# Transposing attention weights by DMA instead of TensorE, with exponentials emitted earlier, in a top-k attention + MLP kernel

## The chip, the cores and the metric

The kernel runs on one core of a Trainium2 chip. The core has a matrix engine (PE, whose weight loads the profile lists as PEld), a vector engine (DVE), an activation engine (ACT), GpSimd (POOL) and a sync engine (SP), whose queue issues the DMAs. Each engine works off its own queue in order and waits on semaphores. The metric is device time in microseconds of one execution; lower is better.

## What is computed

Shapes: q, k and v are (8, 8, 576, 64), that is 8 batches of 8 heads; `w_in` is (512, 2048) and `w_out` (2048, 512), all float32.

```python
scores = scale * q @ k.T                        # 576 x 576 per head
kth    = np.partition(scores, -32)[..., -32]    # the 32nd largest of a row
scores = np.where(scores >= kth, scores, -1e9)
attn   = exp(scores - max) ; attn /= sum + 1e-9
x      = (attn @ v), heads joined               # 4608 tokens x 512
h      = x @ w_in                               # 4608 x 2048
g      = h if h >= 1, 0 if h <= -1, else (h + 1)**2 / 4
out    = g @ w_out                              # 4608 x 512
```

## The kernel before

**Steps.** Attention is cut into 144 steps. A step treats two sets of 128 query rows (128 queries of two heads, or the 64 left-over queries of four), so that its score tile `s` is 128 x 2 x 576. In a step PE makes the scores (L258, each float32 product is two MATMUL records), ACT copies them from PSUM (`s`, L261). DVE then finds the threshold of each row: it takes the larger of each pair (`more`, L269), four times the eight largest (MAX8, L283) with three MATCH_REPLACE8 between them (L292), then deals with the smaller halves (L297, L300, L301, L304). ACT makes the exponentials (`e`, L287) from the first maximum; DVE multiplies them by the mask and sums them (L312) and takes the reciprocal (L318). In the first 12 steps the reciprocals go into a diagonal matrix (`diag`, L322), and PE transposes and scales in one product (L342, L349). In the other 132 POOL scales the weights (L325), and PE transposes them block by block against the identity (L344 eight blocks, L352 one), with ACT copying the result to SBUF (`wT`, `wTt`, L345, L353). PE multiplies with v (L364, L372), and ACT copies the result to `xT` (L377).

**MLP.** When a chunk of one or two 128-token tiles is done, `hidden` makes 16 blocks of h in PSUM (`ph`, L394). ACT makes `r` and `g` from it (L398, L412), POOL finishes the activation with three instructions (L413 to L415), `final` multiplies with `w_out` (`py`, L422), ACT copies (L426) and SP stores. Only the very last chunk uses ACT and DVE instead of POOL (L403 to L405).

**Order.** The order on PE, DVE, ACT and POOL is written out by hand: a Python loop over the steps m, seven slots in each. `weights` is a generator whose yields spread a step's DVE work over the slots, `begin_at` emits scores, `transpose_w` and `values_until` the transposes and the products with v, and `advance` takes MLP work from the queue `pending`. A planner keeps estimated clocks: `dve_time` (a step takes `K_TIME`), `pe_time` (an MLP unit takes `UNIT_TIME`), and `until`, the time of the slot. While the MLP weights are being prepared (`early`, the first 12 steps), scores and values come in slots 4 and 2; later they both come at the start of a step. SP issues in the order written, too.

Of the kernel before, what the change touches and what calls it, by code (L numbers as in the profile page):

```python
# [10 lines left out]
F32 = mybir.dt.float32  # L11
U32 = mybir.dt.uint32
# [11 lines left out]
def kernel(  # L24
# [23 lines left out]
    SH = S // 2  # L48
    NK = DM // P
# [11 lines left out]
    nc.gpsimd.memset(minus, -1.0)  # L61
    two = const.tile([P, 1], F32, name="two")
# [32 lines left out]
    def load(pool, i):  # L95
        if i < n_pieces and i not in loaded:
            if room and i < 28:
                loaded[i] = room[i % 8]
            else:
                loaded[i] = pool.tile([P, 2 * WC], U32, name="raw", bufs=3)  # L100
            nc.sync.dma_start(out=loaded[i], in_=pieces_of_weights[i][1].bitcast(U32))

    def words_of(pool, i):
        load(pool, i)
        words = loaded.pop(i).rearrange("p (n t) -> p n t", t=2)
        return words[:, :, 0], words[:, :, 1]
# [31 lines left out]
    def inspect_piece(pool, i):  # L138

        _, hi = words_of(pool, i)  # L140
        for x in range(2):
            sign = pool.tile([P, WC], F32, name="sign", bufs=3)
# [4 lines left out]
    def run(ctx, paired):  # L147
        xtp = ctx.enter_context(tc.tile_pool(name="xtp", bufs=3))
        stage = ctx.enter_context(tc.tile_pool(name="stage", bufs=2))
        att = ctx.enter_context(tc.tile_pool(name="att", bufs=2))  # L150
        ps = ctx.enter_context(tc.tile_pool(name="ps", bufs=1, space=PSUM))
# [119 lines left out]
        def weights(st, after):  # L271
            s, m = st["s"], st["m"]
            tops = att.tile([P, 2, TOP_K + 8], F32, name="tops", bufs=3)
            st["e"] = e = att.tile([P, 2, S], F32, name="e")
            nmax = att.tile([P, 2], F32, name="nmax")
            kth = att.tile([P, 2, 8], F32, name="kth", bufs=3)
# [4 lines left out]
            for r in range(0, TOP_K, 8):  # L281
                for i in range(2):
                    nc.vector.max(out=tops[:, i, r:r + 8], in_=src[:, i, :])  # L283
                if r == 0:
                    nc.scalar.activation(nmax, tops[:, :, 0], AF.Copy, scale=-1.0)
                    for i in range(2):
                        nc.scalar.activation(e[:, i, :], s[:, i, :], AF.Exp, bias=nmax[:, i:i + 1])  # L287
                        if i == 0:
                            yield
                if r + 8 < TOP_K:  # L290
                    for i in range(2):
                        nc.vector.match_replace(out=rest[:, i, :], in_to_replace=tops[:, i, r:r + 8],  # L292
                                                in_values=src[:, i, :], imm_value=LOWEST)
                    src = rest
                yield
# [12 lines left out]
            if paired and after is not None:  # L308
                pairs(after)
# [9 lines left out]
            if st["by_tensor"]:  # L319
                st["rz"] = diag = att.tile([P, 2, P], F32, name="diag", bufs=1)  # L320
# [12 lines left out]
        def transpose_w(st):  # L333
            w = st["e"]
            st["wT"] = wT = att.tile([P, 2, NT, P], F32, name="wT", bufs=1)
            st["wTt"] = wTt = att.tile([P, P], F32, name="wTt", bufs=1)
            for i in range(2):
                pt = ps.tile([P, NT, P], F32, name="pw", tag="a", bufs=4)
                for c in range(NT):
                    w_in_place = w[:, i, main(i)][:, c * P:(c + 1) * P]  # L340
                    if st["by_tensor"]:
                        nc.tensor.matmul(pt[:, c, :], w_in_place, st["rz"][:, i, :], start=True, stop=True)  # L342
                    else:
                        nc.tensor.transpose(pt[:, c, :], w_in_place, ident)  # L344
                nc.scalar.copy(wT[:, i], pt)  # L345
            pt = ps.tile([P, P], F32, name="pwt", tag="a", bufs=4)
            if st["by_tensor"]:
                for i in range(2):
                    nc.tensor.matmul(pt[i * TL:(i + 1) * TL, :], w[:, i, tail(i)], st["rz"][:, i, :],  # L349
                                     start=True, stop=True)  # L350
            else:
                nc.tensor.transpose(pt, w.rearrange("p i n -> p (i n)")[:, SM:SM + P], ident)  # L352
            nc.scalar.copy(wTt, pt)  # L353


        def values(st):
            t, hp, v_in, v_tl = st["t"], st["hp"], st["keys"]["v"], st["keys"]["v_tl"]
            wT, wTt = st["wT"], st["wTt"]
            po = ps.tile([P, P], F32, name="po", tag="ph", bufs=3)
            if t < NT:  # L360
                for c in range(NT + 1):
                    for j in range(2):
                        h = 2 * hp + j
                        nc.tensor.matmul(po[j * D:(j + 1) * D], v_in[:, h, c, :] if c < NT else v_tl[0][:, h, :],  # L364
                                         wT[:, j, c, :] if c < NT else wTt, start=(c == 0), stop=(c == NT))
            else:
                for i in range(2):
                    cols = slice(i * TL, (i + 1) * TL)
                    for c in range(NT + 1):
                        for j in range(2):  # L370
                            h = 2 * (hp + i) + j
                            nc.tensor.matmul(po[j * D:(j + 1) * D, cols], v_in[:, h, c, :] if c < NT else v_tl[1][:, h, :],  # L372
                                             wT[:, i, c, j * TL:(j + 1) * TL] if c < NT else wTt[:, j * TL:(j + 1) * TL],
# [14 lines left out]
        def mlp(xT, tiles, pool, last):  # L388
            gs, pys = {}, {}

            def hidden(f, c0, c1):
# [6 lines left out]
                nc.scalar.activation(r, ph, AF.Relu, bias=half, scale=0.5)  # L398
# [3 lines left out]
                if last:  # L402
                    nc.vector.tensor_scalar(g, ph, -1.0, 0.0, ALU.add, ALU.max)  # L403
                    nc.scalar.activation(r, r, AF.Square)
                    nc.vector.scalar_tensor_tensor(out=g, in0=r, scalar=1.0, in1=g, op0=ALU.min, op1=ALU.add)  # L405
                    return
                if converted < n_pieces and f % 2:
                    nc.scalar.activation(r, r, AF.Square)
                    nc.scalar.activation(g, ph, AF.Relu, bias=minus, scale=1.0)
                    nc.gpsimd.tensor_scalar(r, r, 1.0, 0.0, ALU.min, ALU.max)  # L410
                else:
                    nc.scalar.activation(g, ph, AF.Relu, bias=minus, scale=1.0)  # L412
                    nc.gpsimd.tensor_scalar(r, r, 1.0, 0.0, ALU.min, ALU.max)  # L413
                    nc.gpsimd.tensor_tensor(out=r, in0=r, in1=r, op=ALU.mult)  # L414
                nc.gpsimd.tensor_tensor(out=g, in0=r, in1=g, op=ALU.add)  # L415
# [26 lines left out]
        for b in range(0, B, 2):  # L442
# [4 lines left out]
            else:  # L447
                rounds += a + [tl, (b + 1, NT)] + c
                chunks += [a[0:2], a[2:4], [tl], c[0:2], c[2:3], c[3:4]]
# [9 lines left out]
        EARLY_CHUNKS = 4  # L459
# [110 lines left out]
        for i in range(2):  # L570
            load(mlp_pool, i)
# [134 lines left out]
```

## Time and profile before

| | |
|---|---|
| median of 3 runs | 1746.03 us (1745.57 to 1747.68) |
| profiled execution: its own time | 1746.35 us |
| profiled execution: span of the instructions | 1744.5 us, mean granted PE clock 0.982 |
| busy: PE, DVE, ACT, POOL | 1639.4, 1537.0, 1083.2, 946.9 us |
| DMA | 74.63 MB, q1 14.5% of 16 engines' span |

Busy times are unions of the records of an engine, so a busy engine can still be waiting in part. A wait is read from the side of the engine that stands idle: "DVE e L312 <- ACT e L287" is time in which DVE had nothing else to do than wait for ACT's line 287.

### The profile page before, as it was taken

The numbers are of one execution on the slowest core, as the hardware profiler recorded it, in microseconds if no ns is written. First come the engines' busy times: TensorE is split into PE (matmuls) and PEld (weight loads), VectorE is DVE, ScalarE is ACT, GpSimd is POOL, SyncE is SP. The second block draws the span as 40 slices with busy tenths as digits, with TensorE's granted clock in tenths as the row PEclk, the third lists the DMA queues.
The fourth block names the chain that finished last, engine by engine and source line by source line (L and its number), as shares of the span: only waits on it lengthen the run. The fifth ranks groups of instructions, "written<-read, shape, count | busy, mean of one in ns | idle before, by whom it ended". The sixth has DMA issues, their size and how long they took to land.

```text
span 1744.5 us, 33535 instructions
## 1 busy us (share of the span) xinstructions
PE 1639.4 (94%) x10665; PEld 1151.5 (66%) x10665; DVE 1537.0 (88%) x4875; ACT 1083.2 (62%) x2942; POOL 946.9 (54%) x1668
## 2 busy tenths in 40 slices
PE   5588989999999999999999999999999999999998
PEld 4476575667766757476756767567667666666665
DVE  7999979888899999999987999999997998899752
ACT  6688575676667857576655647556555555466452
POOL 5689183665544817264646645436365554555550
PEclk7799999999999999999999999999999999999999
DMA  8333112111121112111200101000010000000000
GB/s 253 116 98 97 46 30 65 44 43 41 42 63 52 44 49 65 46 49 41 62 13 22 25 22 44 17 24 17 23 39 19 19 10 14 13 7 7 7 7 15
DMA packets 116668, 74.63 MB, mean 43 GB/s; under 512 B 87296, under 2 KB 95488, under 8 KB 116480
## 3 DMA queue, kind: packets, MB, share of 16 engines
q1 hardware_dynamic: 116480, 72.37, 14.5%
q8 instruction: 87, 1.43, 0.3%
q14 instruction: 101, 0.83, 0.2%
HBM read 62.91 MB, written 9.44 MB: 41 GB/s over the span
## 4 chain that ended last, share of the span: by engine, by line
PE 65%; DVE 14%; POOL 11%; ACT 6%; issue 3%; DMA 0%; POOLq 0%; DVEq 0%; SPq 0%; ACTq 0%
PE py L422 25%; PE ph L394 18%; PE sp L258 7%; PE po L364 7%; PE pw L344 5%; DVE tops L283 4%; DVE more L292 3%; POOL g L415 3%; POOL r L414 3%; DVE e L312 3%; POOL e L325 2%; POOL r L413 2%; ACT s L261 1%; DVE seconds L300 1%; ACT r L398 1%
## 5 line engine op out<-in xcount | busy, mean ns | idle before, releaser
L394 PE MATMUL ph<-xT,w_in 128*128 128x128 f32 (+1 forms) x3200 | 558.0, 326 | 14.4 <-ACT g L412 13.2
L422 PE MATMUL py<-w_out,g 128*128 128x512 f32 x1152 | 530.9, 600 | 2.0 <-ACT y L426 2.0
L394 PEld LDWEIGHTS ph<-xT,w_in 128*128 128x128 f32 x3200 | 472.3, 192 | 87.9 <-ACT g L412 26.0
L325 POOL TENSOR_SCALAR e<-e,rz 128x576 f32<-128x576 f32 x264 | 195.0, 750 | 520.2 <-DVE rz L318 488.8
L283 DVE MAX8 tops<-more 128x8 f32<-128x288 f32 x1152 | 465.4, 445 | 0.0
L292 DVE MATCH_REPLACE8 more<-tops,more 128x288 f32<-128x288 f32 x864 | 375.6, 442 | 0.0
L422 PEld LDWEIGHTS py<-w_out,g 128*128 128x128 f32 x1152 | 205.2, 190 | 224.1 <-issue 215.8
L312 DVE SCALAR_TENSOR_TENSOR e<-s,kth,e 128x576 f32<-128x576 f32 x288 | 245.7, 881 | 116.6 <-ACT e L287 116.3
L398 ACT ACTIVATE r<-ph,half 128x128 f32<-128x128 f32 (+1 forms) x400 | 166.5, 416 | 216.8 <-POOL g L415 156.7
L415 POOL TENSOR_TENSOR g<-r,g 128x128 f32<-128x128 f32 (+1 forms) x384 | 255.9, 666 | 30.2
L413 POOL TENSOR_SCALAR r<-r 128x128 f32<-128x128 f32 (+1 forms) x368 | 173.2, 471 | 132.0 <-ACT r L398 131.7
L414 POOL TENSOR_TENSOR r<-r 128x128 f32<-128x128 f32 (+1 forms) x368 | 213.9, 581 | 30.7
L261 ACT ACTIVATE s<-sp 128x288 f32<-128x288 f32 x576 | 195.2, 421 | 56.8 <-PE sp L258 36.8
L287 ACT ACTIVATE e<-s,nmax 128x576 f32<-128x576 f32 x288 | 213.4, 770 | 7.7
L364 PEld LDWEIGHTS po<-wT,v_in 128*64 128x64 f32 x2048 | 111.8, 137 | 87.9 <-issue 53.2
L258 PE MATMUL sp<-kT,qT 64*128 64x288 f32 x1024 | 163.9, 437 | 4.2 <-ACT kT L218 2.3
L364 PE MATMUL po<-wT,v_in 128*64 128x128 f32 x2048 | 145.5, 280 | 18.7 <-ACT g L412 11.3
L345 ACT COPY wT<-pw 128x512 f32<-128x512 f32 x288 | 154.0, 589 | 13.1 <-PE pw L344 10.6
L344 PEld LDWEIGHTS pw<-ident,e 128*128 128x128 f32 x1056 | 122.2, 142 | 60.0 <-issue 24.4
L344 PE MATMUL pw<-ident,e 128*128 128x128 f32 x1056 | 141.0, 276 | 16.2 <-ACT s L261 10.4
L377 ACT COPY xT<-po 128x128 f32<-128x128 f32 x128 | 34.1, 266 | 195.8 <-PE po L364 195.5
L412 ACT ACTIVATE g<-ph,minus 128x128 f32<-128x128 f32 (+1 forms) x368 | 153.6, 417 | 0.0
(91 smaller groups left out, 1595.1 us busy)
## 6 DMA issues: line engine op xcount, KB each, us to landing
raw<-in_moe_w_out_dram SPq DMA_DIRECT2D x64, 256.0 KB, 2.6
raw<-in_moe_w_in_dram SPq DMA_DIRECT2D x36, 256.0 KB, 2.7
k_in<-in_k_dram SPq DMA_DIRECT2D x64, 128.0 KB, 2.9
q_in<-in_q_dram SPq DMA_DIRECT2D x32, 256.0 KB, 3.1
v_in<-in_v_dram SPq DMA_DIRECT2D x8, 1024.0 KB, 5.8
out_dram<-y SPq DMA_DIRECT2D x32, 256.0 KB, 2.3
kT<-in_moe_w_in_dram SPq DMA_DIRECT2D x16, 256.0 KB, 4.0
v_in<-in_moe_w_in_dram SPq DMA_DIRECT2D x12, 256.0 KB, 4.5
```

The costliest lines, as they stand in the source:

```text
L258: nc.tensor.matmul(o[:, a0 - c0:a1 - c0], qT[d, g, :], kT[d, g, k0:k0 + a1 - a0], start=True, stop=True)
L283: nc.vector.max(out=tops[:, i, r:r + 8], in_=src[:, i, :])
L287: nc.scalar.activation(e[:, i, :], s[:, i, :], AF.Exp, bias=nmax[:, i:i + 1])
L292: nc.vector.match_replace(out=rest[:, i, :], in_to_replace=tops[:, i, r:r + 8], in_values=src[:, i, :], imm_value=LOWEST)
L312: nc.vector.scalar_tensor_tensor(out=e[:, i, :], in0=s[:, i, :], scalar=last[:, i:i + 1], in1=e[:, i, :], op0=ALU.is_ge, op1=ALU.mult, acc ...
L325: nc.gpsimd.tensor_scalar(e[:, i, :], e[:, i, :], rz[:, i:i + 1], 1.0, ALU.mult, ALU.mult)
L344: nc.tensor.transpose(pt[:, c, :], w_in_place, ident)
L364: nc.tensor.matmul(po[j * D:(j + 1) * D], v_in[:, h, c, :] if c < NT else v_tl[0][:, h, :], wT[:, j, c, :] if c < NT else wTt, start=(c == ...
L394: nc.tensor.matmul(ph, w_in[:, kk, f * P:(f + 1) * P], xT[:, kk, c0:c1], start=(kk == 0), stop=(kk == NK - 1))
L414: nc.gpsimd.tensor_tensor(out=r, in0=r, in1=r, op=ALU.mult)
L415: nc.gpsimd.tensor_tensor(out=g, in0=r, in1=g, op=ALU.add)
L422: nc.tensor.matmul(py, gs[f][:, i * P:(i + 1) * P], w_out[:, f, :], start=(f == 0), stop=(f == NF - 1))
```

## The change

Four things are done. From step 12 on (except in the last two steps), the transposes on PE with their copies are replaced: ACT splits the scaled weights into low and high 16-bit halves (`halves`), SP stores these in DRAM (`rows`), and a transposing DMA brings them back as `wT`, its 16-bit halves side by side again. The last two steps use the diagonal matrix. Second, each step's first maximum and its exponentials are emitted in the middle of the step before (`first_top`), and scores and values move from the start of a later step to its slot 4. Third, the activation is made from u = relu(h + 1) and c = min(u/2, 1) as c(u - c), with one ACT instruction on PSUM in place of two, and three POOL instructions as before. Fourth, the planner: later MLP work goes by `pe_time` against DVE's planned time alone, with `K_TIME` 10.2; a new chunk's hidden blocks are put among the `final` work that is still waiting; the last two batches use chunks of one tile, and `EARLY_CHUNKS` goes from 4 to 3.

```diff
+        def first_top(st):
+            s = st["s"]
+            if paired:
+                pairs(st)
...
+            for i in range(2):
+                nc.vector.max(out=tops[:, i, 0:8], in_=(st["more"] if paired else s)[:, i, :])
+            nc.scalar.activation(nmax, tops[:, :, 0], AF.Copy, scale=-1.0)
+            for i in range(2):
+                nc.scalar.activation(e[:, i, :], s[:, i, :], AF.Exp, bias=nmax[:, i:i + 1])
+                yield
...
-            for r in range(0, TOP_K, 8):
+            for r in range(8, TOP_K, 8):
+                for i in range(2):
+                    nc.vector.match_replace(out=rest[:, i, :], in_to_replace=tops[:, i, r - 8:r],
+                                            in_values=src[:, i, :], imm_value=LOWEST)
+                src = rest
+                if r == 8:
+                    yield
+                if r + 8 == TOP_K:
+                    yield
+                    yield from first_top(after) if after is not None else (None, None)
                 for i in range(2):
                     nc.vector.max(out=tops[:, i, r:r + 8], in_=src[:, i, :])
...
-            if paired and after is not None:
-                pairs(after)
...
+        def move_w(st):
+            st["wT"] = wT = late.tile([P, BLOCKS, P], F32, name="wT", bufs=2)
+            halves = late.tile([P, 2, 2 * S], U16, name="halves")
+            for i in range(2):
+                nc.scalar.copy(halves[:, :, i * S:(i + 1) * S], st["e"][:, i, :].bitcast(U16).rearrange("p (k t) -> p t k", t=2))
+            rows = dram.tile([P, 2, 2 * S], U16, name="rows")
+            nc.sync.dma_start(out=rows, in_=halves)
+            nc.sync.dma_start_transpose(wT.bitcast(U16), rows.rearrange("p t k -> (p t) k"))
...
                 else:
-                    nc.scalar.activation(g, ph, AF.Relu, bias=minus, scale=1.0)
-                    nc.gpsimd.tensor_scalar(r, r, 1.0, 0.0, ALU.min, ALU.max)
-                    nc.gpsimd.tensor_tensor(out=r, in0=r, in1=r, op=ALU.mult)
-                nc.gpsimd.tensor_tensor(out=g, in0=r, in1=g, op=ALU.add)
+                    nc.scalar.activation(g, ph, AF.Relu, bias=one)
+                    nc.gpsimd.tensor_scalar(r, g, 0.5, 1.0, ALU.mult, ALU.min)
+                    nc.gpsimd.tensor_tensor(out=g, in0=g, in1=r, op=ALU.subtract)
+                    nc.gpsimd.tensor_tensor(out=g, in0=g, in1=r, op=ALU.mult)
...
-                chunks += [a[0:2], a[2:4], [tl], c[0:2], c[2:3], c[3:4]]
+                chunks += [[x] for x in a + [tl] + c]
...
-        EARLY_CHUNKS = 4
+        EARLY_CHUNKS = 3
...
-        K_TIME, PIECE_TIME, UNIT_TIME, SLOTS, EARLY_STEPS, EARLY_SHARE = 9.6, 0.55, 0.22, 7, 4, 20
+        K_TIME, PIECE_TIME, UNIT_TIME, SLOTS, EARLY_STEPS, EARLY_SHARE = 10.2, 0.55, 0.218, 7, 4, 20
...
+            pe_time = max(pe_time, until - 4.0)
...
-                if not (counted and due >= cost or pe_time < until and (fill or not is_hidden)):
+                if not (not fill and counted and due >= cost or pe_time < until and (fill or not is_hidden)):
...
-                    pending.extend(hiddens(i0, i1) + rest + [work for i in range(i0, i1) for work in finals(i)])
+                    new = hiddens(i0, i1)
+                    if i0 == 0 and ch >= EARLY_CHUNKS and not rest:
+
+                        places = []
+                        while pending and not pending[-1][3] and len(places) < NF // 2:
+                            places.append(pending.pop())
+                        for x, work in enumerate(reversed(places)):
+                            pending.append(work)
+                            upto = (x + 1) * NF // len(places)
+                            pending.extend(new[x * NF // len(places):upto])
+                        new = [] if places else new
+                    pending.extend(new + rest + [work for i in range(i0, i1) for work in finals(i)])
...
-            if not early:
-                values_until(m - 1)
-                begin_at(m + 2)
...
-                parts = [1] * SLOTS if early else [1, 2, 2, 2, 0, 0, 0]
+                parts = [1] * SLOTS
...
-                state[m]["by_tensor"] = early
+                state[m]["by_tensor"] = early or m >= n - 2
...
-                if slot == 1 + (not early) and 1 <= m <= n:
-                    pe_time = max(pe_time, done[m - 1] + 2.0) + 1.0
-                    transpose_w(state[m - 1])
-                    transposed = pe_time
+                if slot == 1 and 1 <= m <= n:
+                    if state[m - 1]["by_tensor"]:
+                        pe_time = max(pe_time, done[m - 1] + 2.0) + 1.0
+                        transpose_w(state[m - 1])
+                        ready_at[m - 1] = pe_time + 1.8
+                    else:
+                        move_w(state[m - 1])
+                        ready_at[m - 1] = done[m - 1] + 13.0
...
-                if slot == 4 and early:
+                if slot == 4:
                     begin_at(m + 2)
+                    if not early:
+                        values_until(m - 1)
```

## Prediction

> **What bounds the kernel now.** I read the page's busy line first, then busy time by stretches, then the waits, then timelines of a late step and of the end.
>
> ```profile
> PE 1639.4 (94%) x10665; PEld 1151.5 (66%) x10665; DVE 1537.0 (88%) x4875; ACT 1083.2 (62%) x2942; POOL 946.9 (54%) x1668
> ```
>
> PE looks like the bound, but DVE is 207.5 us short of the span (1744.5 - 1537.0) and may be the next. The stretches (length; then busy time and instructions of PE, PEld, DVE, ACT, POOL; clock, DMA share, GB/s) cut the run at the twelfth and the last reciprocal, and show single late steps:
>
> ```profile
> 0.00:174.00 174.00, 123.73 (x888) 99.15 (x889) 160.97 (x482) 133.65 (x366) 129.53 (x214) 0.86 0.48 141
> 174.00:1691.90 1517.90, 1469.90 (x9538) 1023.12 (x9537) 1365.14 (x4358) 934.62 (x2534) 813.12 (x1446) 1.00 0.12 33
> 1691.90:1744.50 52.60, 45.76 (x242) 29.18 (x240) 10.86 (x37) 14.88 (x43) 4.30 (x10) 0.97 0.04 13
> ...
> 709.60:719.80 10.20, 9.21 (x54) 5.18 (x53) 9.93 (x35) 5.77 (x17) 1.64 (x3) 1.00 0.19 51
> ...
> 1400.50:1412.20 11.70, 11.70 (x78) 9.76 (x77) 11.43 (x34) 8.68 (x23) 11.05 (x17) 1.00 0.01 2
> 1337.80:1353.90 16.10, 14.46 (x115) 12.51 (x114) 10.34 (x35) 10.52 (x33) 13.35 (x31) 0.89 0.08 18
> ```
>
> The reader is to see three kinds of late step. With POOL quiet DVE fills a step of 10.2 us; with POOL full the same DVE work takes 11.4; and in the last line the step is 16.1 us though DVE has 10.3 to do. In the 132 late steps PE is busy 97%, DVE 90%. The waits say for what DVE stands (total, times, longest):
>
> ```profile
> DVE e L312 <- ACT e L287: 116.3, 80, 6.3
> ```
>
> DVE waits for the exponentials, nothing else of weight. ACT makes them late because it works in order behind MLP work: "ACT r L398 <- POOL g L415" is 156.7 us, and PE's queue is full besides. So PE, POOL's bursts and ACT's order jointly hold DVE up by 116.3 us; without that DVE itself is the limit.
>
> **The change part by part.** *Transposes off PE.* The late block on PE:
>
> ```profile
> 899.36 1.98 PE L422 MATMUL py<-w_out,g 128*128 128x512 f32 x4
> ...
> 901.18 1.04 PE L344 MATMUL pw<-ident,e 128*128 128x128 f32 x8
> ...
> 902.05 0.27 PE L352 MATMUL pwt<-ident,e 128*128 128x128 f32 x1
> ...
> 902.16 1.88 PE L422 MATMUL py<-w_out,g 128*128 128x512 f32 x4
> ```
>
> Products of L422 come every 0.43 us (timeline), so without the block the second group would start at 899.36 + 4 x 0.43 = 901.08; the block costs 902.16 - 901.08 = 1.08 us. For 130 steps (132 less the last two) PE is relieved of 140 us, plus up to 16.2 us of idle before L344: late PE work falls from 1469.9 to about 1325. That saves nothing beyond DVE's own limit.
>
> *ACT.* Gone per step: two copies of 589 ns and one of 288 (L345, L353), 1.47 us. New: two copies of 1152 16-bit elements. Nearest rows: L287 on 576 elements, 770 ns; L412 grows from 369 to 470 ns over 128 elements, 0.79 ns each, so 770 + 576 x 0.79 = 1225 ns; ends 770 (halves at half price) and 1540 (twice the row). I take 1.23, since it is built from two rows: 2.45 us a step, net +1.0, 127 us in all. L412 goes: 368 x 417 ns = -153.6. ACT stays near 1060 us, 64% of a shorter span; at 1540 ns it is some 1140.
>
> *POOL.* Still three instructions a block. L414 (581 ns, one tensor read twice) becomes a product of two, at most L415's 666: 368 x 0.085 = 31 us. One-tile chunks in the last two batches and one two-tile chunk earlier add at most (2 x 1.40 - 2.07) x 48 = 35. POOL reaches about 1010, 61%. By DVE's row the collisions with POOL are 1365.1 - 132 x 9.9 = 58 us; 7% more work makes that 62. +4 us.
>
> *Exponentials earlier.* The first maximum and both exponentials are emitted in slots 2 and 3 of the step before; their user L312 comes in slot 4 of the step itself, about 10 us later. The longest wait was 6.3 us, so the 116.3 go. In ACT's queue they are moved past a step's MLP instructions and the next step's scores. Late next could be the scores: they move from a step's start to slot 4, and `pairs` of the next step's slot 2 needs them: planned at 4/7 x 10.2 = 5.8 us of a step, done 3 to 4 us later (0.43 + 1.2 on PE, 1.7 on ACT in the timeline), needed at 10.2 + 4.5 (after three MATCH_REPLACE8 pairs and two MAX8 pairs). Some 5 us of room, where before there was over a step. New waits there cost between nothing and the old 116; I take 15, as room of 5 us covers all but the longest waits of the list above.
>
> *DVE's own order.* Nothing leaves DVE, but work that covered gaps is moved. Late DVE groups show idle 13.6 us before L300 (a maximum directly behind a pair operation; 132 times, 0.10 us) and 4.5 before L304 (0.034). L283 behind `pairs`, and L312 behind L304, now have the same neighbours: 0.13 x 132 = 17 us. Ends: nothing, or twice.
>
> *DMA, and the new wait on SP.* 576 KB go out and come back per step. Rows:
>
> ```profile
> q1 hardware_dynamic: 116480, 72.37, 14.5%
> ...
> raw<-in_moe_w_out_dram SPq DMA_DIRECT2D x64, 256.0 KB, 2.6
> ...
> v_in<-in_v_dram SPq DMA_DIRECT2D x8, 1024.0 KB, 5.8
> ```
>
> Between 256 and 1024 KB a KB costs (5.8 - 2.6)/768 = 4.2 ns, so 576 KB land in 3.9 us, of which 2.4 is moving. No row shows a transposing DMA. Per packet q1 took 0.145 x 16 x 1744.5 us / 116480 = 34.7 ns. Lower end: it moves like a plain load, 2.4 us. Upper end: if it moved in pieces of 32 bytes at that packet price, 18432 x 34.7 / 16 = 40 us. With 256-byte pieces (128 columns of a row) it is 2304 x 34.7 / 16 = 5.0 us; I take this, nearest to `k_in`, which comes in 256-byte rows, 128 KB in 2.9 us. The Trainium skill, "VectorE: DVE Perf Modes", section "The three transpose paths", speaks against the change: 390 ns on TensorE against 1309 ns by DMA for a 128x128 block of 16 bits; 18 such blocks one after the other would be an estimated 23.6 us a step, and the kernel some 3300 us. "DMA: Bandwidth & Descriptors", "Latency and other measured facts", gives 261 GB/s, 2.3 us by an estimate, and the forecast as it stands.
>
> The queues per step then carry 2.4 + 5.0 + old traffic 0.145 x 10.7 = 9.0 us, under a step of 10.7. Latency: POOL 1.5, ACT 2.5, out 3.9, back 5.0 + 1.5, handing over 1: 15.4 us from a step's end; values are due 1 + 4/7 steps of 10.7 later, 16.8. A longer chain first delays only PE, and by the order (values, MLP work, next scores, `pairs`) a step is at least (latency + 7.5)/3: up to 24 us costs nothing. SP holds the transpose back until the store has landed; behind it wait loads of queries, keys and weight pieces and output stores, 4 us, all issued a step or more ahead. ACT's split waits for POOL's scaling; behind it stand scores and exponentials, covered by the room above.
>
> *The end.* What follows the last reciprocal is mostly fixed:
>
> ```profile
> 1709.60 14.45 PE L394 MATMUL ph<-xT,w_in 128*128 128x128 f32 x128
> ...
> 1723.89 13.90 PE L422 MATMUL py<-w_out,g 128*128 128x512 f32 x32
> 1737.83 0.59 ACT L426 COPY y<-py 128x512 f32<-128x512 f32 x1 [13.03 <-PE py L422]
> ```
>
> Only 1709.6 - 1691.9 = 17.7 us ahead of it can shrink, half of which is old L422 work. The diagonal route took 7.1 us in an early step (reciprocal at 43.6 to L377's end at 50.7); with 5 us of unfinished work it is 12.1: -5.6.
>
> **Sum**, in the profiled execution: 1744.5 - 116.3 + 15 + 17 + 4 - 5.6 = 1658.6; 1.85 lies outside the span (1746.35 - 1744.5) and the median is 0.3 below that run: 1660 us. PE needs 1325 of 1437 late us, 92%.
>
> **The rivals.** *DMA becomes the bound* (slower). The store, the transpose and other traffic share the queues; the transpose has no row. Before, a late step took 1517.9/132 = 11.5 us; so it decides from 11.5 - 2.4 - 1.6 = 7.5 us of moving on, 1.5 times my value. At twice, 10 us, a step takes 14: 174 + 132 x 14 + 52 = 2074 us; at the upper end far more. For it: the 40 us end. Against: the queues are 88% idle in the late stretch.
>
> *Half a gain.* ACT now waits in order for POOL's scaling, which in a POOL burst stands behind MLP work (in the 16.1 us step POOL is busy 13.35), and the scores have less room. If half of the 116.3 returns, 58 in place of 15, it is 1703; range 1690 to 1740. For it: the 80 waits sit in such bursts. Against: the activation's ACT part no longer writes into POOL's two `r` buffers, and hidden blocks are spread among final ones.
>
> *Better than the sum:* no new gaps and waits, a tail of 44 us: 1744.5 - 116.3 - 8.6 + 1.5 = 1621, down to 1610 if POOL's spreading lowers the collisions.
>
> **How the numbers follow.** The forecast (1621 to 1690) has 0.66, half a gain 0.16, DMA 0.13, better than the sum 0.05. Faster is forecast, nearly all of half a gain, and the best case: 0.86; the border between half a gain and none, within 0.2% (3.5 us, about what a measurement of this kernel tells from no change): 0.01; slower 0.13. The range 1615 to 1722 holds the forecast, most of half a gain and the top of the best case, some 0.8.
>
> **What would show it.** Right: DVE busy about the same 1540 us but over 92% of the span; L312's wait for L287 under 15 us; the L344 group gone, PE under 93%; two ACT copies near 1.2 us a step; transposing DMAs of 5 to 8 us to landing; DVE idle of about 0.1 us before L283. Wrong: PE waiting at L364 for a DMA in every step, or SP unable to issue (DMA); DVE idle before `more` or L312 for ACT, with ACT waiting for POOL's `e` (half a gain); a quiet step far from 10.3 us breaks the sum itself.

## The result and the profile after

The changed kernel takes 1793.31 us (median of 4 runs, 1792.94 to 1794.75) against 1746.04 us of the kernel before: a ratio of 1.0271, 95% interval 1.0253 to 1.0288. It is slower by 2.7%, where 1660 us was forecast. The profiled execution took 1793.22 us, with a span of 1791.4.

From the page of the changed kernel, the busy line, the granted clock in 40 slices, the total of the main DMA queue, and the chain that ended last by engine:

```profile
PE 1572.1 (88%) x9773; PEld 1087.3 (61%) x9773; DVE 1568.5 (88%) x4875; ACT 1097.9 (61%) x2480; POOL 1199.5 (67%) x1761
...
PEclk7699999987799999979889999998899999999999
...
q1 hardware_dynamic: 438880, 225.75, 47.1%
...
DVE 45%; POOL 24%; PE 17%; ACT 6%; issue 6%; DMA 1%; SPq 0%; POOLq 0%; DVEq 0%; ACTq 0%
```

PE was relieved as planned (1639.4 to 1572.1). POOL was not at 1010 as the sum had it but at 1199.5, and a quarter of the chain that ended last now runs through it. DVE still has 88%: it was not let go.

The same kernel by stretches, in the columns of before, cut at the twelfth and the last reciprocal, and then three late steps:

```profile
0.00:179.30 179.30, 126.71 (x888) 101.12 (x889) 163.93 (x484) 131.58 (x353) 131.96 (x210) 0.84 0.47 134
179.30:1723.20 1543.90, 1384.73 (x8569) 945.77 (x8568) 1393.99 (x4355) 948.04 (x2078) 1052.08 (x1521) 0.94 0.50 131
1723.20:1791.40 68.20, 60.66 (x319) 40.40 (x318) 10.61 (x37) 18.32 (x51) 15.46 (x31) 0.97 0.04 14
774.00:784.40 10.40, 5.89 (x34) 4.23 (x34) 10.08 (x34) 7.24 (x18) 1.63 (x3) 0.51 0.57 161
398.10:418.00 19.90, 15.91 (x83) 7.63 (x82) 10.62 (x34) 12.16 (x27) 13.96 (x27) 1.00 0.34 105
1444.30:1455.00 10.70, 10.70 (x78) 7.78 (x77) 10.40 (x33) 7.31 (x17) 9.92 (x17) 1.00 0.49 133
```

The fourth line is a quiet step: DVE fills it, as forecast, in 10.4 us. The sixth is a step full of MLP work that also runs well, 10.7 us. The fifth is where the time goes: 19.9 us long, though DVE has 10.6 to do, with POOL busy for 14.0.

Set against the forecast's own sum, term by term (us):

| term | forecast | measured | difference |
|---|---|---|---|
| to the twelfth reciprocal | 174.0 | 179.3 | +5.3 |
| late, DVE busy | 1365.1 + 4 = 1369.1 | 1394.0 | +24.9 |
| late, DVE idle | 1517.9 - 1365.1 - 116.3 + 15 + 17 = 68.5 | 1543.9 - 1394.0 = 149.9 | +81.4 |
| after the last reciprocal | 47.0 | 68.2 | +21.2 |
| span | 1658.6 | 1791.4 | +132.8 |

Before, DVE was idle for 152.8 us of the late stretch (1517.9 - 1365.1); now it is 149.9. What was taken away at one place stands at another. The 46.9 us by which the span grew against the kernel before are elsewhere: 28.9 more of DVE's busy time in the late stretch (1394.0 - 1365.1), 15.6 more after the last reciprocal, 5.3 more before the twelfth, and 2.9 less of idle time. From the groups of the page, and from the list of waits (total, times, longest):

```profile
L325 DVE SCALAR_TENSOR_TENSOR e<-s,kth,e 128x576 f32<-128x576 f32 x288 | 248.4, 899 | 0.4
...
L274 DVE TENSOR_TENSOR more<-s 128x576 f32<-128x576 f32 x144 | 112.5, 781 | 108.4 <-ACT s L266 108.2
```

```profile
POOL e L338 <- DVE rz L331: 301.4, 43, 10.7
ACT halves L366 <- POOL e L338: 220.2, 64, 10.5
...
DVE more L274 <- ACT s L266: 108.2, 35, 9.0
POOL r L433 <- ACT g L432: 108.0, 32, 12.1
```

L325 (L312 before) stands idle for 0.4 us in all, where it waited 116.3 for the exponentials. The pair maximum at L274 waits 108.2 us for the scores. The timeline of the 19.9 us step shows the order (start, duration, idle before it):

```profile
398.09 0.17 DVE L331 RECIPROCAL rz<-z 128x2 f32<-128x2 f32 x1
...
399.37 1.24 PE L263 MATMUL sp<-kT,qT 64*128 64x288 f32 x8
...
402.73 0.64 POOL L433 TENSOR_SCALAR r<-g 128x128 f32<-128x128 f32 x1
...
403.45 0.45 POOL L434 TENSOR_TENSOR g<-g,r 128x128 f32<-128x128 f32 x1
...
403.98 0.46 POOL L435 TENSOR_TENSOR g<-g,r 128x128 f32<-128x128 f32 x1
...
404.42 1.47 POOL L338 TENSOR_SCALAR e<-e,rz 128x576 f32<-128x576 f32 x2
...
405.20 2.20 ACT L366 COPY halves<-e 128x1152 uint16<-128x1152 uint16 x2 [10.51 <-POOL e L338]
...
407.54 1.44 ACT L288 ACTIVATE e<-s,nmax 128x576 f32<-128x576 f32 x2
...
409.90 1.28 ACT L266 ACTIVATE s<-sp 128x288 f32<-128x288 f32 x4
...
411.22 1.20 DVE L274 TENSOR_TENSOR more<-s 128x576 f32<-128x576 f32 x1 [8.97 <-ACT s L266]
```

The scale is ready at 398.3. POOL, in order, still has MLP blocks of three instructions each to finish (the last is shown) and scales the weights at 404.42. ACT, in order too, stands at its first copy into halves; of its 10.5 us of waiting 6.9 lie after 398.3, the others before the scale was there. Behind that copy stand the exponentials and the scores' move out of PSUM, whose products were done at 400.6. DVE gets them at 411.2 and has stood for 9.0. It is the forecast's rival "half a gain", link by link, only at nearly the whole price: 108.2 of the old 116.3.

What made POOL late is one instruction. By shape, the first POOL instruction of a block, in the kernel before (L413, two of its shapes) and after (L433):

```profile
L413 POOL TENSOR_SCALAR r<-r 128x256 f32<-128x256 f32 x176 | 98.6, 560 | 65.1 <-ACT r L398 64.8
...
L413 POOL TENSOR_SCALAR r<-r 128x128 f32<-128x128 f32 x192 | 74.6, 389 | 66.9 <-ACT r L398 66.9
```

```profile
L433 POOL TENSOR_SCALAR r<-g 128x128 f32<-128x128 f32 x256 | 192.4, 752 | 50.6 <-ACT g L432 41.3 <-PE ph L413 9.0
L433 POOL TENSOR_SCALAR r<-g 128x256 f32<-128x256 f32 x144 | 161.0, 1118 | 66.9 <-ACT g L432 66.7
```

Same engine, same kind of instruction, same sizes, but another pair of operations and twice as long: 752 against 389 ns and 1118 against 560. In all 353.4 against 173.2 us.

### The profile page after: what moved, and what is told of

Same layout as the page of the kernel before. It is cut to its first block, busy times and chain, and to the rows that moved or that the text cites. A ratio compares the mean times of both kernels' runs of the same rounds, so it can differ in the third digit from the quotient of the medians.

```text
span 1791.4 us, 30819 instructions
## 1 busy us (share of the span) xinstructions
PE 1572.1 (88%) x9773; PEld 1087.3 (61%) x9773; DVE 1568.5 (88%) x4875; ACT 1097.9 (61%) x2480; POOL 1199.5 (67%) x1761
## 4 chain that ended last, share of the span: by engine, by line
DVE 45%; POOL 24%; PE 17%; ACT 6%; issue 6%; DMA 1%; SPq 0%; POOLq 0%; DVEq 0%; ACTq 0%
DVE more L301 10%; DVE tops L310 9%; POOL r L433 8%; PE py L442 8%; DVE e L325 7%; POOL g L435 6%; POOL g L434 6%; PE ph L413 6%; DVE more L312 4%; DVE seconds L315 4%; DVE tops L285 3%; POOL e L338 3%; DVE more L274 3%; PE sp L263 2%; ACT halves L366 2%
## 5 line engine op out<-in xcount | busy, mean ns | idle before, releaser
L413 PE MATMUL ph<-xT,w_in 128*128 128x128 f32 (+1 forms) x3456 | 575.2, 323 | 33.3 <-ACT g L432 18.6
L413 PEld LDWEIGHTS ph<-xT,w_in 128*128 128x128 f32 x3456 | 515.1, 199 | 119.3 <-issue 40.8
L433 POOL TENSOR_SCALAR r<-g 128x128 f32<-128x128 f32 (+1 forms) x400 | 353.4, 884 | 117.4 <-ACT g L432 108.0
L366 ACT COPY halves<-e 128x1152 uint16<-128x1152 uint16 x260 | 288.3, 1153 | 222.5 <-POOL e L338 220.2
L310 DVE MAX8 tops<-more 128x8 f32<-128x288 f32 x864 | 349.0, 445 | 0.0
L435 POOL TENSOR_TENSOR g<-g,r 128x128 f32<-128x128 f32 (+1 forms) x400 | 266.8, 667 | 31.4
L434 POOL TENSOR_TENSOR g<-g,r 128x128 f32<-128x128 f32 (+1 forms) x400 | 254.7, 637 | 33.4
L432 ACT ACTIVATE g<-ph,one 128x128 f32<-128x128 f32 (+1 forms) x400 | 157.0, 401 | 177.7 <-PE ph L413 176.5
L325 DVE SCALAR_TENSOR_TENSOR e<-s,kth,e 128x576 f32<-128x576 f32 x288 | 248.4, 899 | 0.4
L266 ACT ACTIVATE s<-sp 128x288 f32<-128x288 f32 x576 | 190.5, 411 | 53.5 <-PE sp L263 50.5
L288 ACT ACTIVATE e<-s,nmax 128x576 f32<-128x576 f32 x288 | 215.0, 769 | 4.7
L274 DVE TENSOR_TENSOR more<-s 128x576 f32<-128x576 f32 x144 | 112.5, 781 | 108.4 <-ACT s L266 108.2
L263 PE MATMUL sp<-kT,qT 64*128 64x288 f32 x1024 | 175.9, 455 | 19.9 <-ACT s L266 10.2
L263 PEld LDWEIGHTS sp<-kT,qT 64*128 64x128 f32 x1024 | 98.6, 196 | 96.4 <-issue 50.6
L315 DVE MAX8 seconds<-more 128x8 f32<-128x288 f32 x288 | 118.2, 452 | 14.7 <-POOL r L433 0.5
L312 DVE TENSOR_TENSOR more<-s 128x576 f32<-128x576 f32 x144 | 123.3, 856 | 4.9
```

The lines of the kernel that those rows point to most:

```text
L263: nc.tensor.matmul(o[:, a0 - c0:a1 - c0], qT[d, g, :], kT[d, g, k0:k0 + a1 - a0], start=True, stop=True)
L325: nc.vector.scalar_tensor_tensor(out=e[:, i, :], in0=s[:, i, :], scalar=last[:, i:i + 1], in1=e[:, i, :], op0=ALU.is_ge, op1=ALU.mult, acc ...
L366: nc.scalar.copy(halves[:, :, i * S:(i + 1) * S], st["e"][:, i, :].bitcast(U16).rearrange("p (k t) -> p t k", t=2))
L413: nc.tensor.matmul(ph, w_in[:, kk, f * P:(f + 1) * P], xT[:, kk, c0:c1], start=(kk == 0), stop=(kk == NK - 1))
L433: nc.gpsimd.tensor_scalar(r, g, 0.5, 1.0, ALU.mult, ALU.min)
L434: nc.gpsimd.tensor_tensor(out=g, in0=g, in1=r, op=ALU.subtract)
```

## The experiments

Each was first weighed against the theory that the slower first instruction fills POOL, and that through ACT's order this holds DVE up. The rivals were a loss by the new place of the scores or of the exponentials, by the DMA route, by the chunk list, and by the pace of MLP work. "One run" means a single timed run, without an interval.

**The old activation in the changed kernel** (one run).

```diff
-                    nc.scalar.activation(g, ph, AF.Relu, bias=one)
-                    nc.gpsimd.tensor_scalar(r, g, 0.5, 1.0, ALU.mult, ALU.min)
-                    nc.gpsimd.tensor_tensor(out=g, in0=g, in1=r, op=ALU.subtract)
-                    nc.gpsimd.tensor_tensor(out=g, in0=g, in1=r, op=ALU.mult)
+                    nc.scalar.activation(r, ph, AF.Relu, bias=half, scale=0.5)
+                    nc.scalar.activation(g, ph, AF.Relu, bias=minus, scale=1.0)
+                    nc.gpsimd.tensor_scalar(r, r, 1.0, 0.0, ALU.min, ALU.max)
+                    nc.gpsimd.tensor_tensor(out=r, in0=r, in1=r, op=ALU.mult)
+                    nc.gpsimd.tensor_tensor(out=g, in0=r, in1=g, op=ALU.add)
```

> The changed kernel with the activation of the kernel before (two ACT instructions on PSUM, min-max, square and add on POOL). Theory 1: POOL's busy time about 960 us, its first instruction near 389 and 560 ns, ACT 150 us busier (1250), time 1660-1720. Rival 2 gives the same POOL times, since the instruction is in place again, so a difference from the run with the swapped operations tells them apart. Rival 3: above 1760 in spite of the faster POOL.

It took 1714.23 us: 79 us less than the changed kernel, and 31 less than the kernel before (1745.25 in that batch). From its page the busy line and the first POOL instruction, then its late stretch, then DVE's main wait:

```profile
PE 1547.6 (90%) x9773; PEld 1072.3 (63%) x9773; DVE 1550.5 (91%) x4875; ACT 1214.7 (71%) x2880; POOL 986.1 (58%) x1761
...
L434 POOL TENSOR_SCALAR r<-r 128x128 f32<-128x128 f32 (+1 forms) x400 | 165.4, 413 | 196.3 <-ACT r L432 194.7
```

```profile
176.80:1643.20 1466.40, 1357.50 (x8558) 927.86 (x8557) 1378.30 (x4355) 1058.39 (x2450) 846.26 (x1516) 0.96 0.52 138
```

```profile
DVE more L274 <- ACT s L266: 46.7, 18, 9.6
```

ACT does 117 us more and POOL 213 less, and the kernel is faster: the saving on ACT was bought on the engine that others wait for. For the same 400 blocks the first instruction takes 165.4 us instead of 353.4; these 188 us are nearly all that POOL had beyond the forecast's 1010 (1199.5 - 1010 = 190). The wait for the scores falls from 108.2 to 46.7, and DVE's busy time by 15.7 in the late stretch. Most of the loss against the forecast is the activation (79 of 133 us); the rest of the change gains 1.8% on the kernel before.

**The new activation alone in the kernel before** (one run; the reverse edit, with before's order, transposes and pace).

> The kernel before with the new activation alone. Theory 1: POOL's busy time goes from 947 to about 1190 us, its bursts, which were already near full, get longer, and the time goes from 1746 to 1800-1880. Rival 3 (the activation is harmless, the loss comes from the moved scores and from ACT's wait for POOL): 1725-1755, since ACT loses 154 us of work.

1834.61 us, 89 slower than before, with POOL at 1176.2 us and this wait:

```profile
DVE e L314 <- ACT e L289: 172.1, 87, 10.5
```

The same activation costs 79 to 89 us in either frame. Here DVE stands where it stood before, at the exponentials (172.1 against 116.3); in the changed kernel it stands at the scores.

**The same product with its two steps exchanged** (4 runs).

```diff
-                    nc.gpsimd.tensor_scalar(r, g, 0.5, 1.0, ALU.mult, ALU.min)
+                    nc.gpsimd.tensor_scalar(r, g, 2.0, 0.5, ALU.min, ALU.mult)
```

> The changed kernel with the two operations of POOL's first activation instruction in the other order: r = min(g, 2) * 0.5 in place of min(g * 0.5, 1), the same value. Theory 1 (the pair multiply-then-minimum is slow on POOL, and POOL's bursts then hold up ACT and DVE): the instruction falls from 752 ns (128 columns) and 1118 ns (256) to under 450 and 650, POOL's busy time from 1199 to about 1020 us, DVE's wait for the scores (108 us) to under 30, and the time to 1650-1700. Rival 2 (it is slow because it reads one tile and writes another, or because a multiplication stands in it at all): 752 and 1118 ns stay, and so does 1793. Rival 3 (ACT's in-order wait for POOL's scaling and the clumps of hidden blocks are the cause, however fast POOL is): POOL gets faster, but the time stays above 1760.

1792.95 us, ratio to before 1.0268 (1.0251 to 1.0286): no change from the kernel under study. The instruction by shape:

```profile
L433 POOL TENSOR_SCALAR r<-g 128x128 f32<-128x128 f32 x256 | 193.6, 756 | 50.7 <-ACT g L432 47.3 <-PE ph L413 3.2
```

So it does not matter which of the two operations comes first. What in the instruction is slow was left to the next run.

**Eight ways to write the first instruction** (one run). The old activation, but its clamp written in another way in each eighth of the blocks (by `f % 8`), always in place on `r`. The cut shows the five forms whose times stand below.

```diff
+                    x = f % 8
+                    if x == 0:
+                        nc.gpsimd.tensor_scalar(r, r, 1.0, 1.0, ALU.mult, ALU.mult)
+                        nc.gpsimd.tensor_scalar(r, r, 1.0, 0.0, ALU.min, ALU.max)
...
+                        nc.gpsimd.tensor_scalar(r, r, 1.0, 1.0, ALU.mult, ALU.min)
+                    elif x == 3:
+                        nc.gpsimd.tensor_scalar(r, r, 1.0, 0.0, ALU.min, ALU.max)
+                    elif x == 4:
+                        nc.gpsimd.tensor_scalar(r, r, 1.0, None, ALU.min)
+                    elif x == 5:
+                        nc.gpsimd.tensor_scalar(r, r, 0.0, 1.0, ALU.max, ALU.min)
```

> Which property makes POOL's first activation instruction slow. The changed kernel with the old activation, where POOL's tensor_scalar is written in eight ways by block number, all in place on r and all of the same value (r is not negative): mult-mult before a min-max, min-mult, mult-min, min-max (as before), min alone, max-min, add-min, min-min. If a pair of a product or sum with a minimum is slow (theory 1b): min-mult, mult-min and add-min take about 630 ns at least on 128 columns, min-max, max-min, min-min, min alone and mult-mult about 290. If any product is slow: mult-mult and min-mult too, add-min not. If reading one tile and writing another was slow (rival 2): all eight near 290 at least, since all are in place. The total should be near 1714 plus some 40 us.

1777.31 us, more than I had summed, since forms that I expected to be quick were slow. Five of the groups by shape, in the order mult-min, max-min, min alone, mult-mult, min-max:

```profile
L441 POOL TENSOR_SCALAR r<-r 128x128 f32<-128x128 f32 x34 | 27.1, 798 | 3.6 <-ACT r L432 3.3
...
L447 POOL TENSOR_SCALAR r<-r 128x128 f32<-128x128 f32 x30 | 21.4, 714 | 3.5 <-ACT r L432 3.5
...
L445 POOL TENSOR_SCALAR r<-r 128x128 f32<-128x128 f32 x34 | 20.2, 594 | 5.3 <-ACT r L432 5.3
...
L436 POOL TENSOR_SCALAR r<-r 128x128 f32<-128x128 f32 x34 | 13.4, 394 | 51.2 <-ACT r L432 51.2
L443 POOL TENSOR_SCALAR r<-r 128x128 f32<-128x128 f32 x30 | 12.8, 427 | 0.4 <-ACT r L432 0.4
```

Min-mult took 759 ns, add-min 726, min-min 694. On 256 columns the two quick pairs took 545 to 641 ns and the others 910 to 1342. The cost of this instruction depends on its pair of operations, and of the eight, two pairs are quick. Neither the separate input and output, which the new form has and this run has not, nor the product is the cause; even max-min, the old clamp turned round, is slow. Nor is it collisions with other engines: the shortest single execution of the quick pairs took 287 to 294 ns, that of min alone 525, and those of the other five 635 to 643. Why a pair is quick or slow, no run shows.

**The late transposes back on PE** (one run; old activation, the rest as changed: eight transposes into two PSUM tiles, one of the tails, three ACT copies in place of the halves and the two DMAs).

> The changed kernel with the old activation, and the late transposes back on PE (eight blocks and a tail against the identity, three ACT copies, no split, no DMA); the order of everything else is kept. If relieving PE of 1.08 us a step is what the DMA path brings: PE's late work rises by 140 us, to more than the steps leave, and the time goes from 1714 to 1750-1800. If PE has room by now and the DMA path brings nothing: 1700-1725, as ACT loses 0.9 us a step.

1772.46 us, 58 more than the run with the old activation and the DMA route. PE's busy time is 1651.8 (93%), and `DVE more L274 <- ACT s L266` is 80.9 us instead of 46.7. In this frame the DMA route is the part that earns: without it the kernel is 27 us slower than the one before (1745.21 in that batch). The 58 us may be more than its worth, because the transposes on PE are new work that the planner does not count here (`move_w` adds nothing to `pe_time`), while the kernel before counted it; a planner that knows of them was not tried.

**Scores at the start of their step again**, with the new activation (one run). Only the place of the scores' products and moves is undone.

```diff
+            if not early:
+                begin_at(m + 2)
...
-                if slot == 4:
+                if slot == 4 and early:
```

> The changed kernel, its activation kept, with the next scores emitted at the start of a step again, as in the kernel before, in place of slot 4. If DVE's 108 us of waiting for the scores come from their short lead (ACT's copies of the scores stand behind its in-order wait for POOL's scaling, in slot 1): that wait falls under 30 us, and the time goes from 1793 to 1700-1740, although POOL's slow instruction stays. If POOL's bursts hold DVE up in any order (the wait moves to the exponentials or PE): 1775-1800.

1783.18 us, 10 less. The waits of DVE:

```profile
DVE seconds L315 <- POOL excess L340: 35.1, 14, 5.3
...
DVE more L274 <- ACT s L266: 30.1, 16, 4.3
DVE e L325 <- ACT e L288: 20.9, 24, 1.4
```

The wait for scores falls by 78 us and two others appear: L315 writes `seconds`, which a POOL instruction behind the MLP blocks (L340) has still to read, and the exponentials are late again. The span is 10.0 us shorter: with POOL this full, the new order mostly changes where DVE stands.

**Both: old activation and scores at the start** (4 runs). This is the best kernel of the study.

> The changed kernel with the old activation and the scores at the start of a step. If both causes are as I think: DVE's wait for the scores falls from 47 to under 15 us, the late steps take 10.4 to 11.4 us, and the time is 1660-1690. If only the activation mattered: 1705-1725.

1703.34 us (1702.88 to 1705.51), ratio to before 0.9761 (0.9744 to 0.9777). Its late stretch, DVE's wait for the scores, and the engines of its chain that ended last:

```profile
176.80:1630.90 1454.10, 1362.04 (x8550) 910.08 (x8549) 1380.63 (x4357) 1056.56 (x2448) 847.58 (x1514) 0.97 0.52 140
```

```profile
DVE more L274 <- ACT s L266: 21.6, 8, 5.9
```

```profile
PE 65%; DVE 15%; ACT 8%; POOL 7%; issue 3%; DMA 2%; POOLq 0%; SPq 0%; DVEq 0%; ACTq 0%
```

The chain is PE's again, 65% as in the kernel before, with DVE idle for 73.5 us of the late stretch (1454.1 - 1380.6). That is about the forecast's own 68.5. In the list of waits 28.2 of them are for ACT (21.6 for the scores, 6.6 for the exponentials); the other 45.3 are short gaps ahead of DVE's own instructions, 36.5 before (152.8 - 116.3).

**The exponentials back in their own step** (one run; old activation, scores as in the change): the pair maximum (L274), the first maximum and the exponentials are called at the top of `weights`, not in the step before.

> The changed kernel with the old activation, and pairs, first maximum and exponentials at the start of their own step, so that the exponentials have no lead of half a step. If that lead is worth what I forecast for it: DVE waits 60-116 us for the exponentials at the mask, and the time goes from 1714 to 1760-1800. If the lead is worth nothing, because the later scores take it back: 1705-1725.

1712.35 us against 1714.23. With the scores in slot 4 the half-step lead is worth nothing: `DVE e L325 <- ACT e L288` is then 27.3 us in 13 waits, and the wait for the scores, 46.7 us with the lead, is gone from the list, since the pair maximum, which needs them, also comes half a step later. With the scores at the start of the step the lead was not tested.

**One-tile chunks throughout** (one run; new activation).

```diff
-                chunks += [a[0:2], a[2:4], c[0:2], c[2:4], [tl]]
+                chunks += [[x] for x in a + c + [tl]]
```

> The changed kernel with one-tile chunks throughout, as its last two batches have, and POOL's slow instruction kept. Theory 1 with the clumps as its carrier: a tile needs 16 x 1.84 us of POOL in four steps of 10.8, so no stretch is bound by POOL; the late steps all take about 10.8 us as they do from 1401 to 1714 us, and the time is 179 + 132 x 10.8 + 68 = about 1675. If the DMA or the PE clock were the cause instead, the batches would not differ and the time would stay above 1760.

1883.35 us: the worst of all, where I had expected a gain. I had read the smooth stretch at 1401 to 1714 us as the merit of small chunks. They cost POOL 110 us more (1309.6), and the wait for the scores doubled:

```profile
DVE more L274 <- ACT s L266: 212.0, 60, 9.0
```

A block of one tile takes POOL 1.8 us and a block of two 2.8, so small chunks are the dearer way to the same work.

**The pace of MLP work, and the end** (the first two one run each, the third 4 runs, the fourth one run). First the old activation with a step planned at 10.8 us instead of 10.2; then MLP work given out by its due share alone instead of to the planned end of the step; then the best kernel at 10.8; then the best kernel with the old chunk list in the last two batches.

```diff
-        K_TIME, PIECE_TIME, UNIT_TIME, SLOTS, EARLY_STEPS, EARLY_SHARE = 10.2, 0.55, 0.218, 7, 4, 20
+        K_TIME, PIECE_TIME, UNIT_TIME, SLOTS, EARLY_STEPS, EARLY_SHARE = 10.8, 0.55, 0.218, 7, 4, 20
```

> The changed kernel with the old activation and K_TIME 10.8 in place of 10.2, near the measured step. The end after the last reciprocal is 69 us there, 22 more than I had forecast. If the planner's short step holds MLP work back that PE could do (theory: too little work is handed out per step, so more than a tile is left over): PE gets 6% more per step, the end shrinks to 50-58 us and the time to 1690-1705. If PE has no room in the last steps: the end stays at 65-70, and denser hidden blocks make the clumps worse: 1715-1740.

> The changed kernel with the old activation and late MLP work given out by the share that falls due (spread to the next chunk's arrival) instead of as fast as the planned PE clock allows. If clumps of hidden blocks (POOL 2.0 us a block against 1.74 on PE), with ACT waiting in order for POOL's scaling, make the 52 us for which DVE still waits: that falls under 25, PE no longer runs dry, its clock rises from 0.947 to over 0.97, time 1670-1700. If not: 52 us stay, and the time is 1705 or more.

> The same version (old activation, scores at the start) with K_TIME 10.8. With the scores at slot 4 this setting shortened the end from 69 to 58 us and added 75 us of waits for the scores. If these waits came from the scores' short lead, they are gone here, only the shorter end is left, and the time is 1685-1697. If a longer planned step makes POOL's clumps denser in any order: 1715-1780.

> The version with the old activation and the scores at the start of a step (1703), with the old chunks in the last two batches (two tiles, except the last two and the left-over rows). If the one-tile chunks leave the long end (70 us after the last reciprocal, where I had forecast 47), since their hidden blocks come one by one between final work at the pace of the steps: the end shrinks to 52-58 us and the time to 1685-1695. If the end is long because MLP work arrives in lumps just before the last two batches, whatever the chunks: 65-72 us stay, and clumps of two-tile blocks add some waits: 1700-1730.

With a step planned at 10.8 the end shrinks about as expected (58.4 from 69.2 us after the last reciprocal), but the time rises to 1787.51, with 116.9 us of waits for scores; in the best kernel the same setting gives an end of 58.9 and 1760.3 us, ratio to before 1.0086 (1.0069 to 1.0103), with 74.3 us of these waits. The due share gave 1719.65 (1714.23 without it). The old chunk list gave 1711.39, and the end grew to 75.6 us. So the long end is not the work of the one-tile chunks, and the slower pace takes 11 us from it but pays more than that in waits before.

## Why the prediction was wrong

The main step that failed is the first sentence on POOL: "Still three instructions a block." I costed the second of the three (31 us) and the chunks (35), and took the first, L413, over at its old 471 ns, though its operations, its input and its output are all changed. With the old activation in its place the 1010 holds: POOL takes 986.1 us there. The slow form adds 188 us on POOL, and the time of the kernel rises by 79 of the 133 us by which the span missed the forecast. The prediction bounded the second instruction, whose form had no row, by the slowest of the three, L415's 666 ns; the first, whose form had no row either, got no bound. It measured 884 (752 and 1118 by shape), above even 666, so that bound would have shown the risk, though not its size. The other 54 us are there with the old activation too: 22 at the end, 20 of DVE's idle time and 9 of its busy time in the late stretch, 3 before the twelfth reciprocal.

The second is the "15" for new waits. I had "half a gain" as a rival with the right links (ACT waiting in order for the scaling, the scaling behind MLP work in a burst) and gave it 58 us and 0.16. It measured 108.2. Its size came from POOL: with the old activation it was 46.7 us, near the 58, and with the scores back at the step's start 21.6, near the 15. "Room of 5 us covers all but the longest waits" held against the old list of waits, not against POOL's new bursts, behind which DVE stands for up to 9.0 us. The 17 us for new short gaps were too many: the idle time before L285 is 4.5 us (the prediction's 0.10 us a step came out at 0.034) and before L325 0.4.

Third, DVE's busy time: +25 us. The forecast's rate for collisions with POOL was 58 us for 813 us of POOL work, 0.071. Taking the old activation back took 205.8 us of POOL's late work and 15.7 of DVE's, 0.076: the rate agrees, and the missed POOL work is the larger part. Some 9 us stay that I did not foresee; they are there with the old activation too (1378.3 against 1369.1).

Fourth, the end: "with 5 us of unfinished work it is 12.1: -5.6" failed by 21 us. PE does 60.66 us of work after the last reciprocal where it did 45.76. The kernels with this pace and this chunk list agree on it (68.2, 69.2, 70.3). The pace is shown to be worth half of it (58.4 and 58.9 with steps planned at 10.8); that the order in which the last chunks become ready is the other half was not tested and stays open. Of the 5.3 us of the early part, 2.5 go with the old activation (176.8), and the rest stays open too.

The rival "DMA becomes the bound" did not come true. The main queue took all 16 engines for 0.471 x 1791.4 = 843.7 us in sum, against 0.145 x 1744.5 = 253.0; that is (843.7 - 253.0) / 130 = 4.5 us a step for the store and the transpose, where 2.4 + 5.0 was forecast. PE's waits for `wT` are small:

```profile
PEld po L383 <- DMA wT<-rows: 34.3, 16, 4.2
...
PE po L383 <- DMA wT<-rows: 24.2, 12, 3.3
```

The rest of the steps held: a quiet step of 10.4 us (forecast 10.3), the waits for exponentials gone, two ACT copies of 1153 ns (1.23 us), and a store of 2.8 us, less than the 3.9 of the sum. With POOL's instruction as it was and the scores where they were, the kernel took 1703 us, inside the range, though not down at 1660: 23 of those 43 us are the end's miss (70.3 against 47.0).

## What to carry to other kernels

An algebraic rewrite that saves an instruction on one engine must be costed on every instruction it changes, the one that keeps its name too: here the same instruction, engine and size took twice the time with another pair of operations. Where two engines work in order and hand over to each other (here POOL's scaling, then ACT's copy, then the scores), a burst on the first is paid by whoever is last in the second one's queue; moving the victim to another slot moved most of the wait along (10 us won of 78 here, while the burst stayed), and what helped most was less work on the first. And when a wait is taken away from the engine that bounds, its idle time over the stretch, not that wait's row, tells whether anything was won.

## What the runs showed of the hardware

- GpSimd's tensor_scalar on 128x128 32-bit numbers took 394 ns as mult-mult and 360 to 458 as min-max (of one run), but 594 to 798 in the six other forms tried, a single min among them; on 256 columns 545 to 641 against 910 to 1342. The cause inside the engine is not shown.
- A transposing DMA of 256 x 1152 16-bit numbers landed in 4.8 us (median of 130), with its store of 576 KB in 2.8:

```profile
rows<-halves SPq DMA_DIRECT2D x130, 576.0 KB, 2.8
...
wT<-rows SPq DMA_TRANSPOSE x130, 4.8
```

  That is 0.27 us for each of 18 blocks of 128x128. The Trainium skill, "VectorE: DVE Perf Modes", section "The three transpose paths", has 1309 ns for one; as the price of each of many in one transfer the measurement decides against it.
- A PE with gaps ran at a lower granted clock: 0.51 in the quiet step at 774 us, with PE busy for 5.89 of 10.40 us, and 0.929 over the whole execution against 0.982 before. The Trainium skill, "TensorE: Matmul & The Clock Gate", "Part 1: The HAM clock gate", states a half rate after at least one idle window of about 3.4 us; the 0.51 agrees with its half, and no run here tests the 3.4. Late PE work was 1384.7 us where 1325 had been forecast; I had not foreseen slower products. How much of the difference is the clock, and what it cost in time, was not measured apart.
